# Moving a router's third token unit beside the attention chunks, and the row writes of four tile pairs back

## The chip, the cores and the metric

The kernel runs on one core of one Trainium2 chip. The core has five instruction queues that run on their own and meet only at semaphores: TensorE (PE in the profile, with its weight loads as PEld), VectorE (DVE), ScalarE (ACT), GpSimd (POOL) and SyncE (SP). The last three also issue the transfers. The metric is the device time of one execution in microseconds (us), as the median of several runs.

## The reference

Two blocks follow each other. The first is gated linear attention over 4 batches, 8 heads, 768 steps and head width 48; its state decays by `alpha` and takes up `k` times `v` at every step:

```python
state = alpha[:, :, t, :, None] * state + np.einsum('bhd,bhe->bhde', k[:, :, t], v[:, :, t])
y[:, :, t] = np.einsum('bhd,bhde->bhe', q[:, :, t], state)
```

Its output, as 3072 rows of 384 numbers, goes to a router with 8 experts. Each row gets noisy logits, `x @ w_gate + log(1 + exp(x @ w_noise)) * noise`; the two best experts are chosen, their softmax weights are the gates, and the row's result is the sum over its two experts of `gate * (relu(x @ w1[e]) @ w2[e])`, with w1 of 384 x 1024 and w2 of 1024 x 384. All of it is float32.

## The kernel before, in words

**Chunks.** The attention runs over 24 chunks of 128 rows, six to a batch. A loop of 23 turns (n from 0 to 22) issues for each turn the pieces of several chunks at different stages: keys, inverses, scaled keys and queries of chunk n + 2, alphas and products of n + 3, the transposed keys of n + 1, the output of n, the state and the masked scores of n + 1. The title of the change counts from 1, so its chunks 19 to 22 are the turns n = 18 to 21. In DVE's queue a turn is, in this order: the scan `over` (L385), the scaled queries `q_P` (L413), the state `S` (L472), two copies under a mask (L445, "masks" below; they write the matrix that L254 on PE multiplies with the values) and the scan `P_all` (L373). POOL multiplies the keys with `over` (L403, `k_P`) and decays the state (L473). The order of the pieces is written out by hand in a string:

```python
ORDER = "keys inverses alphas turn_y turn_k scaled queries block output no_more state scores masked products"
```

A place p of a turn is behind the p-th piece of this string.

**Routing.** The 24 chunks are four units of six. When a unit's chunks are done, `routing(u)` finds for its 768 rows the two best experts (DVE finds the 8 largest and their indices, L742 and L743, two chunks at a step), the gates (ACT: Exp, Ln, Exp, with table loads between), and each row's place in its expert's list. For the place PE multiplies the counts with a triangular and a full matrix of ones (L795, L796, `rank`). Then `enter` computes 12 columns of places (L801 to L820), and POOL writes 12 times 128 entries into a table in memory, one indirect transfer each (L173, "puts" below). The generator is stepped on by hand. `ROUTE[u]` lists for units 0 and 1 the (turn, place) of every step, counted from the turn in which the unit's last chunk is at its third stage; units 2 and 3 are stepped on by times in the second half.

**Pairs.** The second half is 24 pairs of tiles, 256 rows of one expert each, and three smaller tiles. A pair gathers its rows with an indirect transfer (L1008), turns them (PE, or a transposing transfer from pair 2 on), and multiplies them with the weights in fewer products than the plain form, with sums of blocks formed by DVE (L1229, L1232, L1290, L1381, L1385). ACT and DVE gather the result of pair i in `o`, of which there are two: pair i uses the one that pair i - 2 used. POOL writes the rows of `o` out with two plain indirect transfers (L992) and two that add (L1000). Pairs 0 to 4 read lists that units 0 and 1 alone fill; pair 5 needs unit 2, later ones all four.

**What sets the order in the second half.** Each step of a pair has a time on a scale on which a pair lasts T = 20, and all steps are sorted by it: this is the order in which they stand in each engine's queue, and it is no time on the chip. (d, t) below is d * T + t. A put of the second half also waits for the DVE sum that was recorded last before it (`behind`).

Of the kernel before, what the change touches and what calls it, by code (L numbers as in the profile page):

```python
# [19 lines left out]
def kernel(  # L20
# [273 lines left out]
    def fast_gla(on):  # L294
# [210 lines left out]

        ROUTE = (((1, 9), (2, 8), (2, 13), (3, 4), (3, 11), (4, 8), (4, 10), (4, 10), (5, 5), (5, 7)), ((1, 9), (2, 8), (2, 11), (2, 13), (3, 4), (3, 8), (3, 10), (3, 10), (4, 5), (4, 7), (4, 12)))
        routes = [routing(u, on) for u in range(NU)]

        def route(n, place):
            for u in range(2):
                for _ in range(ROUTE[u].count((n - (u + 1) * UC + 1, place))):
                    next(routes[u], None)

# [164 lines left out]
    seen = [const.tile([C, E], F32, name=f"seen{i}") for i in range(2)]  # L680
# [4 lines left out]
    def routing(u, on, planned=True):  # L685
        late = u if planned and u >= NU - 2 else 0
        noisy, lg = noisy_logits(u, on)
        yield
        nc.scalar.activation(noisy, noisy, AF.Ln, bias=1.0)
        yield  # L690
        top, at = best(u, on, lg, noisy, [])
        yield
        for c in range(0, UC - 2, 2):
            if (u, c) in ((NU - 2, 2), (NU - 1, 0)):
                nc.scalar.activation(unread_exp, ones[0:1, 0:1], AF.Exp)
            best(u, on, lg, noisy, range(c, c + 2), top, at)
            yield
        best(u, on, lg, noisy, range(UC - 2, UC), top, at)
        entry, at_f = choose(on, top, at)
        if u < NU - 2:  # L700
            nc.scalar.activation(unread_exp, ones[0:1, 0:1], AF.Exp)
            yield
        gates(entry)
        yield
        picked, counts = choose_rest(u, on, entry, at_f)
        past = count_past(u, on, counts)
        yield
        rank = ranked(u, on, counts, past)
# [53 lines left out]
    def choose_rest(u, on, entry, at_f):  # L762
        rp = on["two"]
        w = entry[:, :, :, 1]
        den = rp.tile([C, UC, 1], F32, name="den")
        nc.vector.tensor_add(den, w[:, :, 0:1], w[:, :, 1:2])
        nc.vector.tensor_scalar(out=den, in0=den, scalar1=1e-9, scalar2=None, op0=ALU.add)
        nc.vector.reciprocal(out=den, in_=den)
        nc.vector.tensor_mul(w, w, den.to_broadcast([C, UC, 2]))
        nc.gpsimd.tensor_copy(out=entry[:, :, :, 0], in_=token_f[:, ds(u * UC, UC), None].to_broadcast([C, UC, 2]))  # L770
        for k in range(2):
            nc.gpsimd.tensor_copy(out=entry[:, :, k, 2], in_=at_f[:, 1 - k, :])

# [7 lines left out]
        (nc.gpsimd if u < NU - 2 else nc.vector).tensor_copy(out=counts[:, :, 0], in_=seen[u % 2])  # L781
        chosen = counts[:, :, 1:].rearrange("p e c -> p c e")
        nc.vector.tensor_tensor(chosen, picked[:, 0], picked[:, 1], op=ALU.add)
        return picked, counts

    def count_past(u, on, counts):
        past = on["two"].tile([C, E, 1 + UC], F32, name="past")
        nc.vector.tensor_tensor_scan(past.rearrange("p e c -> p (e c)"), within.rearrange("p e c -> p (e c)"),
                                     counts.rearrange("p e c -> p (e c)"), 0.0, op0=ALU.mult, op1=ALU.add)
        (nc.gpsimd if u < NU - 2 else nc.vector).tensor_copy(out=seen[(u + 1) % 2], in_=past[:, :, UC])  # L790
        return past

    def ranked(u, on, counts, past):
        rank = few(on, [C, UC, E], "rank", u >= NU - 2)
        nc.tensor.matmul(rank, before, counts[:, :, 1:].rearrange("p e c -> p c e"), start=True, stop=False)  # L795
        nc.tensor.matmul(rank, ones, past[:, :, 0:UC].rearrange("p e c -> p c e"), start=False, stop=True)  # L796
        return rank
# [57 lines left out]
        nc.vector.tensor_scalar(out=short, in0=short, scalar1=float(R2), scalar2=None, op0=ALU.is_lt)  # L855

    def check_third(on):
        total = few(on, [C, E], "total", True)
# [264 lines left out]
    def pairs(on):  # L1123
# [17 lines left out]
        tabs, wheres, lists, bank, puts = {}, {}, {}, {}, {}  # L1141
# [262 lines left out]

        T = 20.0
        FIRST_BEHIND = 2
        PUT_LATER = {1: 13.0, 2: 16.0, 3: 12.0, 4: 6.0}
        EARLY_0 = {"tab": -300.0, "w1": -410.0, "find": -200.0, "gather": -199.0, "w2": -405.0, "join": -100.5, "turn": -100.0,
                   "turned": -100.0, "joined": -100.0, "s0": -1.05, "sum_x": -1.0, "sum_xs": -0.99, "s1": -0.8, "s3": -0.7, "s2": -0.6, "t0": 3.5, "t1": 4.3}
        every = {("w1", 0): 1.0, ("w2", 0): 1.0, ("w1", 1): 1.2, ("w2", 1): 2.0}  # L1410
# [309 lines left out]
    with ExitStack() as es:  # L1720
        on = pools(es, "")
# [8 lines left out]
        def beside():  # L1730
# [7 lines left out]
            left += [(t, lambda: route_on(2)) for t in when((0, 8.95), (0, 12.0), (0, 12.65), (0, 13.1), (0, 17.4), (0, 18.7), (0, 19.96), (1, 3.6), (1, 4.6), (2, 19.0))]  # L1738
            left += [(t, lambda: route_on(3)) for t in when((1, 5.0), (1, 10.2), (2, 5.2), (2, 7.6), (2, 9.7), (2, 9.8), (2, 12.2), (2, 15.2), (2, 17.5))]
            left += [(t, lambda: route_on(3)) for t in when((5, 10.7), (8, 10.7), (9, 1.6), (9, 6.2), (11, 10.7), (11, 20.8), (12, 1.6), (12, 6.2))]  # L1740
            puts = when((1, 6.0), (1, 8.6), (1, 10.1), (1, 12.7), (1, 14.0), (1, 16.6), (1, 19.2), (2, 0.6), (2, 2.6), (2, 5.2), (2, 9.0), (2, 11.4), (2, 17.6), (2, 18.9), (3, 2.6), (3, 3.9), (3, 5.2), (3, 6.5), (3, 8.8), (3, 10.1), (3, 11.4), (3, 12.7), (3, 15.0), (3, 17.3))
            left += [(t, lambda: put_some(1, latest["sum"])) for t in puts]
            assert len(puts) == 4 * UC
            return left

        steps = [pair_steps(i) for i in range(NPAIR)]
# [151 lines left out]
```

## Time and profile before

| | |
|---|---|
| Median of 3 runs | 620.96 us (620.77 to 621.24) |
| The profiled execution | 621.97 us |
| Its span, first to last instruction | 620.3 us |
| PE busy | 607.0 us, 98% |
| PE weight loads busy | 583.7 us, 94% |
| DVE busy | 508.0 us, 82% |
| ACT busy | 330.9 us, 53% |
| POOL busy | 317.4 us, 51% |
| Granted TensorE clock over the span | 0.997 |

The profiled execution is 1.0 us longer than the median. Times inside it are counted from the span's start. The chunks end and the pairs begin at about 153 us; the last products of the pairs end at about 613 us.

### The profile page before, as it was taken

The numbers are of one execution on the slowest core, as the hardware profiler recorded it, in microseconds if no ns is written. First come the engines' busy times: TensorE is split into PE (matmuls) and PEld (weight loads), VectorE is DVE, ScalarE is ACT, GpSimd is POOL, SyncE is SP. The second block draws the span as 40 slices with busy tenths as digits, with TensorE's granted clock in tenths as the row PEclk, the third lists the DMA queues.
The fourth block names the chain that finished last, engine by engine and source line by source line (L and its number), as shares of the span: only waits on it lengthen the run. The fifth ranks groups of instructions, "written<-read, shape, count | busy, mean of one in ns | idle before, by whom it ended". The sixth has DMA issues, their size and how long they took to land.

```text
span 620.3 us, 14271 instructions
## 1 busy us (share of the span) xinstructions
PE 607.0 (98%) x5274; PEld 583.7 (94%) x5274; DVE 508.0 (82%) x1158; ACT 330.9 (53%) x665; POOL 317.4 (51%) x355
## 2 busy tenths in 40 slices
PE   8999999999999999999999999999999999999994
PEld 5899999999999999999999999999999999989894
DVE  8788898988879869968898798887688879878672
ACT  4877868685655334444444544445544445444431
POOL 7353267884137786545434434555347527443254
PEclk9999999999999999999999999999999999999998
DMA  9999999984997854664654837775997678885223
GB/s 144 175 199 223 237 188 175 214 179 106 259 235 145 235 136 128 126 166 121 115 126 105 171 66 200 193 98 132 271 211 199 140 184 221 181 220 118 80 44 55
DMA packets 181552, 101.09 MB, mean 163 GB/s; under 512 B 150088, under 2 KB 172074, under 8 KB 181472
## 3 DMA queue, kind: packets, MB, share of 16 engines
q1 hardware_dynamic: 145056, 35.56, 34.5%
q10 hardware_dynamic: 21280, 44.05, 24.4%
q0 software_dynamic: 15136, 20.47, 14.8%
q8 instruction: 44, 0.72, 0.5%
q14 instruction: 36, 0.29, 0.2%
HBM read 76.41 MB, written 24.22 MB: 162 GB/s over the span
## 4 chain that ended last, share of the span: by engine, by line
PE 81%; DVE 6%; POOL 5%; issue 4%; ACT 2%; DMA 1%; POOLq 0%; ACTq 0%; DVEq 0%
PE sc L1356 19%; PE h_ps L1363 18%; PE o_ps L1363 13%; PE c_ps L1356 8%; PE sc L1348 4%; PE tp L345 3%; PE sc L425 3%; PE y L254 2%; PE h_ps L277 2%; POOL table L173 2%; PE y L493 2%; DVE P_all L373 1%; POOL k_P L403 1%; PE tp L452 1%; PE h_half_ps L1678 1%
## 5 line engine op out<-in xcount | busy, mean ns | idle before, releaser
L992 POOL DMA_INDIRECT out_dram<-o,where x46 | 48.5, 1054 | 166.6 <-DVE o L1381 91.1
L1367 ACT ACTIVATE h<-h 128x512 f32<-128x512 f32 x92 | 56.9, 628 | 78.2 <-DVE h L1229 61.7
L1000 POOL DMA_INDIRECT out_dram<-o,where x44 | 71.0, 1615 | 13.4 <-issue 13.1
L1008 POOL DMA_INDIRECT x_in<-x_rows,where x48 | 58.6, 1220 | 24.4 <-issue 12.7
L1363 PE MATMUL o_ps<-wt,hx 128*128 128x192 f32 x384 | 70.8, 327 | 0.0
L1356 PE MATMUL sc<-yT,ws 128*128 128x128 f32 x480 | 66.6, 275 | 1.5 <-DVE m L1232 1.5
L1356 PEld LDWEIGHTS sc<-yT,ws 128*128 128x128 f32 x480 | 62.9, 191 | 1.8 <-DVE m L1232 1.8
L173 POOL DMA_INDIRECT table<-entry,place_u x48 | 55.0, 1145 | 16.5 <-issue 9.5
L1363 PEld LDWEIGHTS o_ps<-wt,hx 128*128 128x128 f32 x384 | 61.5, 190 | 1.8 <-issue 1.8
L403 POOL TENSOR_TENSOR k_P<-k_P,over 128x512 f32<-128x512 f32 (+1 forms) x24 | 27.7, 1154 | 40.5 <-DVE over L385 32.3
L1223 ACT COPY xt<-x_turned 128x768 uint16<-128x768 uint16 x44 | 43.8, 1053 | 2.1 <-DMA x_turned<-x_in 2.1
L345 PE MATMUL tp<-ident,ins 128*128 128x128 f32 x288 | 42.9, 282 | 1.6 <-ACT k_P L395 0.6
L1377 ACT ACTIVATE o<-h_ps,tab 128x192 f32<-128x192 f32 x46 | 19.4, 421 | 42.7 <-PE h_ps L1363 41.3
L345 PEld LDWEIGHTS tp<-ident,ins 128*128 128x128 f32 x288 | 32.1, 144 | 7.1 <-ACT k_P L395 1.0
L445 DVE COPY_PREDICATED shared<-upto,sc 128x512 f32<-128x512 uint32 x47 | 32.0, 736 | 7.6 <-PE sc L425 7.0
L1488 ACT COPY m<-sc 128x512 f32<-128x512 f32 x20 | 11.7, 586 | 48.0 <-PE sc L1356 48.0
L1363 PE MATMUL h_ps<-wt,h 128*128 128x192 f32 x192 | 35.2, 327 | 0.0
L1363 PE MATMUL o_ps<-w,h 128*128 128x192 f32 x192 | 35.2, 326 | 0.0
L1363 PE MATMUL h_ps<-wt,hx 128*128 128x192 f32 x192 | 35.2, 326 | 0.0
L1363 PE MATMUL h_ps<-w,h 128*128 128x192 f32 x192 | 35.1, 326 | 0.0
L1363 PE MATMUL h_ps<-w,hx 128*128 128x192 f32 x192 | 35.1, 326 | 0.0
L1356 PE MATMUL c_ps<-xs,w 128*128 128x128 f32 x240 | 33.3, 275 | 0.0
(333 smaller groups left out, 1611.9 us busy)
## 6 DMA issues: line engine op xcount, KB each, us to landing
w<-in_moe_w_dram ACTq DMA_DIRECT2D x33, 512.0 KB
w<-in_moe_w_dram ACTq DMA_DIRECT2D x44, 384.0 KB
ins<-in_alpha_dram SPq DMA_DIRECT2D x24, 192.0 KB
ins<-in_k_dram SPq DMA_DIRECT2D x24, 192.0 KB
ins<-in_q_dram SPq DMA_DIRECT2D x24, 192.0 KB
vt<-in_v_dram SPq DMA_DIRECT2D x24, 192.0 KB
x_rows<-y_sb SPq DMA_DIRECT2D x24, 192.0 KB
ins<-in_moe_w_dram ACTq DMA_DIRECT2D x9, 512.0 KB
```

The lines of the kernel that those rows point to most:

```text
L173: put = nc.gpsimd.indirect_dma_start(out=table, out_offset=bass.IndirectOffsetOnAxis(ap=place, axis=0), in_=entry, in_offset=None, bounds_ ...
L345: nc.tensor.transpose(tp[:, j, :], src[:, 2 * j:2 * j + 2, :], ident)
L403: (nc.vector if n == NT - 1 else nc.gpsimd).tensor_tensor(c["k"][:, at], c["k"][:, at], over[:, at, 1:CB], op=ALU.mult)
L445: nc.vector.copy_predicated(MTs[n % 2][:, i], mask_upto, sc)
L992: put = nc.gpsimd.indirect_dma_start(out=out, out_offset=bass.IndirectOffsetOnAxis(ap=at, axis=0), in_=rows, in_offset=None, bounds_check= ...
L1000: add = nc.gpsimd.indirect_dma_start(out=out, out_offset=bass.IndirectOffsetOnAxis(ap=at, axis=0), in_=rows, in_offset=None, bounds_check= ...
L1008: nc.gpsimd.indirect_dma_start(out=rows, out_offset=None, in_=x_rows[0:units * UT, :], in_offset=bass.IndirectOffsetOnAxis(ap=at, axis=0), ...
L1223: nc.scalar.copy(halves[:, part], x_turned[:, :, part].rearrange("p s a t -> p s (a t)"))
L1348: nc.tensor.matmul(bank[name][:, f, :], W[:, ds(f * C, C)], X, start=new and f == 0, stop=True, skip_group_check=True)
L1356: nc.tensor.matmul(bank[name][:, 2 * h + f, :], W[h][:, ds(f * C, C)], X[h], start=new and not h and not f, stop=True, skip_group_check=True)
L1363: nc.tensor.matmul(bank[name], H[:, f, :], W[:, f, :], start=new and f == 0, stop=True, skip_group_check=True)
L1367: nc.scalar.activation(t, t if src is None else src, AF.Relu)
```

## The change

Unit 2 gets a row of its own in `ROUTE`, the same as that of unit 1, so that its eleven steps stand in turns 18 to 21. The ten times at which it was stepped on in pairs 0 to 2 now step unit 3 on; nine are left, and the nine times of unit 3 in pairs 1 and 2 are gone. Where the code asked whether a unit is one of the last two (`u < NU - 2`) it now asks whether it is the last, so unit 2 takes its rank bank from the pool `h`, copies its counts on POOL, and loads the Exp table where units 0 and 1 do. Of unit 2's 12 puts four go in turns 21 and 22 (`put_some(2)` was there and had nothing left to put), eight at eight new times in pair 0. Unit 3's 12 puts take the first twelve of the 24 old times. `PUT_LATER`, by which the row writes of pairs 1 to 4 stood 6 to 16 units later than those of other pairs, is empty.

```diff
-        ROUTE = (((1, 9), ..., (5, 7)), ((1, 9), (2, 8), (2, 11), ..., (4, 12)))
+        ROUTE = (((1, 9), ..., (5, 7)), ((1, 9), (2, 8), (2, 11), ..., (4, 12)), ((1, 9), (2, 8), (2, 11), (2, 13), (3, 4), (3, 8), (3, 10), (3, 10), (4, 5), (4, 7), (4, 12)))
...
-            for u in range(2):
+            for u in range(NU - 1):
...
-            if (u, c) in ((NU - 2, 2), (NU - 1, 0)):
+            if (u, c) == (NU - 1, 0):
...
-        if u < NU - 2:
+        if u < NU - 1:
             nc.scalar.activation(unread_exp, ones[0:1, 0:1], AF.Exp)
             yield
...
-        rank = few(on, [C, UC, E], "rank", u >= NU - 2)
+        rank = few(on, [C, UC, E], "rank", u >= NU - 1)
...
-        PUT_LATER = {1: 13.0, 2: 16.0, 3: 12.0, 4: 6.0}
+        PUT_LATER = {}
...
-            left += [(t, lambda: route_on(2)) for t in when((0, 8.95), (0, 12.0), ..., (1, 4.6), (2, 19.0))]
-            left += [(t, lambda: route_on(3)) for t in when((1, 5.0), (1, 10.2), ..., (2, 17.5))]
+            left += [(t, lambda: route_on(3)) for t in when((0, 8.95), (0, 12.0), ..., (1, 4.6))]
...
-            puts = when((1, 6.0), (1, 8.6), ..., (2, 11.4), (2, 17.6), ..., (3, 17.3))
+            puts = when((0, 0.5), (0, 2.0), ..., (0, 11.0), (1, 6.0), (1, 8.6), ..., (2, 11.4))
...
-            assert len(puts) == 4 * UC
+            assert len(puts) == 4 * UC - 4
```

DVE in turn 20, from the scan `over` of chunk 22 to the masks of chunk 21 (`sc` with two numbers); L1182 begins the row search of pair 0. Before:

```order
L385 SCALAR_TENSOR_TENSOR over<-shared,P_all 128x515
L413 TENSOR_TENSOR q_P<-tp,P_all 128x512
L472 TENSOR_TENSOR S_156<-S_155,o_ps 128x192
L445 COPY_PREDICATED shared<-upto,sc_2352 128x512
L445 COPY_PREDICATED shared<-upto,sc_2353 128x512
L1182 TENSOR_SCALAR tab_2279<-tab_2279 128x2
```

Now there stand three steps of the largest values behind `over`, and behind them, up to the masks:

```order
L754 TENSOR_TENSOR entry<-top 128x12
L766 TENSOR_TENSOR den<-entry 128x6
L767 TENSOR_SCALAR den<-den 128x6
L768 RECIPROCAL den<-den 128x6
L769 TENSOR_TENSOR entry<-entry,den 128x12
L776 TENSOR_TENSOR picked<-expert_idv,at_f 128x96
L783 TENSOR_TENSOR counts<-picked 128x6x8
L788 SCALAR_TENSOR_TENSOR past<-within,counts 128x56
L472 TENSOR_TENSOR S_156<-S_155,o_ps 128x192
L445 COPY_PREDICATED shared<-upto,sc_2396 128x512
L445 COPY_PREDICATED shared<-upto,sc_2397 128x512
```

The state and the masks of chunk 21 stand behind six searches for the largest values, the gates' sums and the counts of unit 2.

DVE in turn 21, from the scan `over` of chunk 23 over the masks of chunk 22. Before:

```order
L385 SCALAR_TENSOR_TENSOR over<-shared,P_all 128x515
L403 TENSOR_TENSOR k_P<-k_P,over 128x512
L472 TENSOR_TENSOR S_155<-S_156,o_ps 128x192
L445 COPY_PREDICATED shared<-upto,sc_2443 128x512
L445 COPY_PREDICATED shared<-upto,sc_2444 128x512
L413 TENSOR_TENSOR q_P<-tp,P_all 128x512
```

Now:

```order
L385 SCALAR_TENSOR_TENSOR over<-shared,P_all 128x515
L403 TENSOR_TENSOR k_P<-k_P,over 128x512
L801 TENSOR_TENSOR picked<-picked,h_ps 128x96
L803 TENSOR_REDUCE place_f<-picked 128x12
L815 TENSOR_SCALAR picked<-place_f 128x2x6
L817 TENSOR_TENSOR picked<-place_f,picked 128x2x6
L820 SCALAR_TENSOR_TENSOR place_u<-at_f,picked 128x12
L472 TENSOR_TENSOR S_155<-S_156,o_ps 128x192
L445 COPY_PREDICATED shared<-upto,sc_2499 128x512
L445 COPY_PREDICATED shared<-upto,sc_2500 128x512
L860 SCALAR_TENSOR_TENSOR short<-h_ps,short 128x1
L413 TENSOR_TENSOR q_P<-tp,P_all 128x512
```

The five instructions of `enter` for unit 2 stand ahead of the state and the masks of chunk 22, and the check of one list's length (L860) behind them.

POOL in pairs 2 and 3, where the rows of pair 1 (`o_186`) and of pair 2 (`o_185`) are written out; L1155 loads a list of three pairs. Before:

```order
L173 DMA table<-entry,place_u 25600x8 x6
L1008 DMA x_in<-x_rows,where_3175 128x768 x2
L173 DMA table<-entry,place_u 25600x8
L992 DMA out_dram<-o_186,where_2463 3072x384
L1000 DMA out_dram<-o_186,where_2463 3072x384
L173 DMA table<-entry,place_u 25600x8
L992 DMA out_dram<-o_186,where_2463 3072x384
L1000 DMA out_dram<-o_186,where_2463 3072x384
L173 DMA table<-entry,place_u 25600x8 x4
L1155 DMA tab_3365<-table 128x6x8
```

Now:

```order
L173 DMA table<-entry,place_u 25600x8 x2
L992 DMA out_dram<-o_186,where_2522 3072x384
L1000 DMA out_dram<-o_186,where_2522 3072x384
L992 DMA out_dram<-o_186,where_2522 3072x384
L1000 DMA out_dram<-o_186,where_2522 3072x384
L1008 DMA x_in<-x_rows,where_3205 128x768 x2
L992 DMA out_dram<-o_185,where_2651 3072x384
L1000 DMA out_dram<-o_185,where_2651 3072x384
L992 DMA out_dram<-o_185,where_2651 3072x384
L1000 DMA out_dram<-o_185,where_2651 3072x384
L1155 DMA tab_3377<-table 128x6x8
```

Of twelve puts in this stretch two are left, ahead of the four row writes of pair 1; the writes of pair 2 now stand ahead of the list.

## Rows read from the trace of the kernel before

**Rows 1.** Windows: stretch, length, busy PE, PEld, DVE, ACT, POOL, clock, DMA, GB/s.

```profile
229.00:242.00 13.00, 11.23 (x87) 10.77 (x86) 10.51 (x21) 5.93 (x11) 8.00 (x8) 1.00 0.40 106
242.00:600.00 358.00, 358.00 (x2717) 349.29 (x2716) 292.28 (x670) 171.02 (x300) 170.63 (x135) 1.00 0.65 153
```

**Rows 2.** Timeline of PE and ACT in pairs 3 and 4: start, us, what, [idle before].

```profile
230.36 1.47 PE L1363 MATMUL h_ps<-wt,hx 128*128 128x192 f32 x8
230.97 0.42 ACT L1377 ACTIVATE o<-o_ps,tab 128x192 f32<-128x192 f32 x1 [3.86 <-DMA out_dram<-o,where]
...
233.36 1.16 PE L1356 MATMUL sc<-yT,ws 128*128 128x128 f32 x8 [1.54 <-DVE m L1232]
...
235.25 1.47 PE L1363 MATMUL h_ps<-wt,h 128*128 128x192 f32 x8
...
236.55 0.61 PE L1356 MATMUL sc<-yT,ws 128*128 128x128 f32 x4
...
240.93 0.68 PE L1356 MATMUL sc<-xt,q_P 128*128 128x128 f32 x4 [0.23 <-ACT h L1367]
```

**Rows 3.** Timeline of DVE where unit 1 is routed, turn 14.

```profile
101.35 1.23 DVE L385 TENSOR_TENSOR_SCAN over<-shared,P_all 128x515 f32<-128x515 f32 x1
102.50 0.14 DVE L742 MAX8 top<-noisy 128x8 f32<-128x8 f32 x1
...
103.17 0.67 DVE L413 TENSOR_TENSOR q_P<-tp,P_all 128x512 f32<-128x512 f32 x1
...
108.25 1.22 DVE L373 TENSOR_TENSOR_SCAN P_all<-shared,least 128x516 f32<-128x516 f32 x1
```

**Rows 4.** Timeline of DVE and POOL in turns 19 to 22.

```profile
135.54 1.37 DVE L445 COPY_PREDICATED shared<-upto,sc 128x512 f32<-128x512 uint32 x2 [0.62 <-issue]
...
136.50 1.21 POOL L403 TENSOR_TENSOR k_P<-k_P,over 128x512 f32<-128x512 f32 x1
...
136.79 2.02 DVE L373 TENSOR_TENSOR_SCAN P_all<-shared,least 128x516 f32<-128x516 f32 x1
...
139.13 1.23 DVE L385 TENSOR_TENSOR_SCAN over<-shared,P_all 128x515 f32<-128x515 f32 x1
...
143.59 0.15 DVE L1182 TENSOR_SCALAR tab<-tab 128x2 f32<-128x2 f32 x1
...
144.14 1.22 DVE L373 TENSOR_TENSOR_SCAN P_all<-shared,least 128x516 f32<-128x516 f32 x1
...
149.12 0.68 DVE L413 TENSOR_TENSOR q_P<-tp,P_all 128x512 f32<-128x512 f32 x1
```

**Rows 5.** Timeline of PE: output products of chunks 21 and 22.

```profile
145.04 1.09 PE L254 MATMUL y<-shared,vt 128*48 128x128 f32 x16
...
149.98 1.09 PE L254 MATMUL y<-shared,vt 128*48 128x128 f32 x16
```

**Rows 6.** Timeline of DVE: `enter` of unit 2 in pair 1, first instruction and the next.

```profile
180.46 0.26 DVE L801 TENSOR_TENSOR picked<-picked,rank 128x96 f32<-128x96 f32 x1
...
181.56 0.25 DVE L722 TENSOR_TENSOR lg<-lgs 128x96 f32<-128x96 f32 x1
```

**Rows 7.** Timeline of PE: rank of unit 1 in turn 15.

```profile
106.52 0.44 PE L795 MATMUL h_ps<-counts,before 128*128 128x48 f32 x2
...
107.16 0.62 PE L345 MATMUL tp<-ident,ins 128*128 128x128 f32 x4
```

**Rows 8.** Timeline of PE: rank of unit 2 in pair 1.

```profile
179.85 0.34 PE L795 MATMUL rank<-counts,before 128*128 128x48 f32 x2
...
180.24 1.12 PE L1348 MATMUL sc<-xt,ws 128*128 128x128 f32 x8
```

**Rows 9.** Timeline: gather of pair 2's rows, and first reading of them turned.

```profile
159.41 1.00 POOL L1008 DMA_INDIRECT x_in<-x_rows,where  x1 [5.88 <-ACT x_turned L288]
...
178.75 1.06 ACT L1223 COPY xt<-x_turned 128x768 uint16<-128x768 uint16 x1
```

**Rows 10.** Waits of PE: us in total, times, longest.

```profile
PE tp L345 <- DVE q_P L413: 0.4, 2, 0.2
```

More of the change, by code (lines that the diff above doesn't have):

```diff
@@ L504, in put_y @@
                 put_rows(n, chunks[n].pop("y"))
-        ROUTE = (((1, 9), (2, 8), (2, 13), (3, 4), (3, 11), (4, 8), (4, 10), (4, 10), (5, 5), (5, 7)), ((1, 9), (2, 8), (2, 11), (2, 13), (3, 4), (3, 8), (3, 10), (3, 10), (4, 5), (4, 7), (4, 12)))
+        ROUTE = (((1, 9), (2, 8), (2, 13), (3, 4), (3, 11), (4, 8), (4, 10), (4, 10), (5, 5), (5, 7)), ((1, 9), (2, 8), (2, 11), (2, 13), (3, 4), (3, 8), (3, 10), (3, 10), (4, 5), (4, 7), (4, 12)), ((1, 9), (2, 8), (2, 11), (2, 13), (3, 4), (3, 8), (3, 10), (3, 10), (4, 5), (4, 7), (4, 12)))
         routes = [routing(u, on) for u in range(NU)]
         def route(n, place):
-            for u in range(2):
+            for u in range(NU - 1):
                 for _ in range(ROUTE[u].count((n - (u + 1) * UC + 1, place))):
@@ L780, in choose_rest @@
         counts = rp.tile([C, E, 1 + UC], F32, name="counts")
-        (nc.gpsimd if u < NU - 2 else nc.vector).tensor_copy(out=counts[:, :, 0], in_=seen[u % 2])
+        (nc.gpsimd if u < NU - 1 else nc.vector).tensor_copy(out=counts[:, :, 0], in_=seen[u % 2])
         chosen = counts[:, :, 1:].rearrange("p e c -> p c e")
@@ L789, in count_past @@
                                      counts.rearrange("p e c -> p (e c)"), 0.0, op0=ALU.mult, op1=ALU.add)
-        (nc.gpsimd if u < NU - 2 else nc.vector).tensor_copy(out=seen[(u + 1) % 2], in_=past[:, :, UC])
+        (nc.gpsimd if u < NU - 1 else nc.vector).tensor_copy(out=seen[(u + 1) % 2], in_=past[:, :, UC])
         return past
     def ranked(u, on, counts, past):
-        rank = few(on, [C, UC, E], "rank", u >= NU - 2)
+        rank = few(on, [C, UC, E], "rank", u >= NU - 1)
         nc.tensor.matmul(rank, before, counts[:, :, 1:].rearrange("p e c -> p c e"), start=True, stop=False)
@@ L857, in check_third @@
     def check_third(on):
-        total = few(on, [C, E], "total", True)
+        total = few(on, [C, E], "total")
         nc.tensor.matmul(total, ones, seen[(NU - 1) % 2], start=True, stop=True)
@@ L1737, in beside @@
             when = lambda *steps: [d * T + t for d, t in steps]
-            left += [(t, lambda: route_on(2)) for t in when((0, 8.95), (0, 12.0), (0, 12.65), (0, 13.1), (0, 17.4), (0, 18.7), (0, 19.96), (1, 3.6), (1, 4.6), (2, 19.0))]
-            left += [(t, lambda: route_on(3)) for t in when((1, 5.0), (1, 10.2), (2, 5.2), (2, 7.6), (2, 9.7), (2, 9.8), (2, 12.2), (2, 15.2), (2, 17.5))]
+            left += [(t, lambda: route_on(3)) for t in when((0, 8.95), (0, 12.0), (0, 12.65), (0, 13.1), (0, 17.4), (0, 18.7), (0, 19.96), (1, 3.6), (1, 4.6))]
             left += [(t, lambda: route_on(3)) for t in when((5, 10.7), (8, 10.7), (9, 1.6), (9, 6.2), (11, 10.7), (11, 20.8), (12, 1.6), (12, 6.2))]
-            puts = when((1, 6.0), (1, 8.6), (1, 10.1), (1, 12.7), (1, 14.0), (1, 16.6), (1, 19.2), (2, 0.6), (2, 2.6), (2, 5.2), (2, 9.0), (2, 11.4), (2, 17.6), (2, 18.9), (3, 2.6), (3, 3.9), (3, 5.2), (3, 6.5), (3, 8.8), (3, 10.1), (3, 11.4), (3, 12.7), (3, 15.0), (3, 17.3))
+            puts = when((0, 0.5), (0, 2.0), (0, 3.5), (0, 5.0), (0, 6.5), (0, 8.0), (0, 9.5), (0, 11.0), (1, 6.0), (1, 8.6), (1, 10.1), (1, 12.7), (1, 14.0), (1, 16.6), (1, 19.2), (2, 0.6), (2, 2.6), (2, 5.2), (2, 9.0), (2, 11.4))
             left += [(t, lambda: put_some(1, latest["sum"])) for t in puts]
-            assert len(puts) == 4 * UC
+            assert len(puts) == 4 * UC - 4
             return left
```

## The prediction

> **What bounds the kernel now.** I read the page's busy shares first, then the windows by stage, then PE's own waits, then the timelines around the two places that the change touches. PE is busy for 98% of the span at the full clock, so only a stretch in which PE stands still can give time back, and everything that makes PE stand still somewhere else costs time. The windows tell where it stands still. From 242 to 600 us PE is busy for all 358 us; from 229 to 242 it is busy for 11.23 of 13 [rows 1]. The reader is to see there that the second half has one hole, and that nothing in the pairs after pair 4 is to be had.
>
> The hole is in pairs 3 and 4. ACT's first write into `o` for pair 3 waits 3.86 us, until 230.97, for the transfer that still reads that `o`: the rows of pair 1 [rows 2]. POOL has 12 puts in that stretch, and the old `PUT_LATER` puts the row writes of pair 1 among them. DVE's sum of pair 4 comes late behind ACT, and PE's step at 233.36 waits for it. Eight products of that shape take 1.30 us (235.25 to 236.55), the eight before the hole take 3.00 (230.36 to 233.36), so 1.70 are lost. A second wait of 0.23 stands at 240.93 [rows 2], where DVE has not caught up; busy rows overhang the next start by 1.47 - 1.30 = 0.17, so it is 0.40. Together 2.1 us. The idle shown in the windows, 1.77, is the floor of this term.
>
> **The change part by part.** *Row writes and puts.* With the puts gone from pairs 2 and 3 and the writes of pair 1 directly behind its last sums, POOL is done with them before pair 3 comes to write, and ACT finds `o` free. I take the whole 2.1 as gained, with 1.8 as the lower end. Nothing takes the hole's place as the next to be late: the windows show no second one behind it.
>
> *Unit 2 beside the chunks.* This costs DVE time in a stage where DVE has little. I follow DVE from turn 19 to the output of chunk 22. The two noise sums of unit 2 stand before the masks of chunk 20, where DVE sits idle for 0.62 [rows 4], and the sum of the logits in a like gap one turn before: nothing. The first step of largest values takes 0.67, as the one between 102.50 and 103.17 for unit 1 [rows 3], and pushes the scan `P_all` at 136.79 to 137.46. That scan took 2.02 before, against 1.22 for the same scan at 144.14; it began 0.29 after POOL's `k_P`, with 0.92 of that to go [rows 4]. Moved, it shares only 0.25 with it. So of the extra 0.80 between none and all may go; I take 0.55, since the overlap shrinks by about that share. `over` then starts at 139.13 + 0.67 - 0.55 = 139.25 (139.0 to 139.8).
>
> What follows `over` is now what followed it for unit 1: two steps of largest values, the entry, the wait for the gates, the counts, the state and the masks. There it took from 101.35 to 108.25, 6.90 us [rows 3]. So the masks of chunk 21 end at 146.15; before they ended at 143.59, where the row search begins [rows 4]. PE wants them at 145.04 [rows 5], had a slack of 1.45, and the masks come 2.56 later. PE has to wait until 146.2, which is 1.15 later than before. The rank products of unit 2 lie inside this: in turn 15 they took 0.64 [rows 7], and PE would have come at 145.68 with them.
>
> The next masks are worse. From the end of the masks of chunk 21 to the end of those of chunk 22 DVE had no gap to speak of: 143.59 to 149.12, 5.53 us [rows 4]. Five instructions of `enter` now stand in between, 1.10 us from 180.46 to 181.56 [rows 6]. So these masks end at 146.15 + 6.63 = 152.8. PE multiplies with them at 149.98 [rows 5], and now at 152.85: 2.9 us later than before. The product that checks a list lies in this wait. From here PE and DVE are late by the same amount: the scaled queries of chunk 23 follow the masks directly, and pair 0's first sums wait for PE's scores as before. So the loss at the chunks is 2.9 us. Its ends: `over` at 139.0 and at 139.8 give 2.6 and 3.4.
>
> *What leaves the pairs.* PE no longer computes the rank of unit 2 in pair 1, 0.39 from 179.85 to 180.24 [rows 8], nor the small check, for which I take half of that: 0.6. DVE's and ACT's part of unit 2 in pairs 0 and 1 does not leave; unit 3's takes its place at the same times. Unit 3's in pairs 1 and 2 does leave, some 6 us of DVE, and gives nothing where PE is never waiting.
>
> *Moved for nothing.* Two puts stand in each of turns 21 and 22 behind the state on POOL; behind them wait the gathers of pairs 0 and 1, which PE sees only through DVE's copies of the rows, and these come later anyway. Five puts now stand ahead of pair 2's gather, at 159.41 before; such a transfer took POOL 1.00 there, so with their issue they are 5 to 7 us. The turned rows are first read at 178.75 [rows 9], so 19 us cover the gather, its landing and the transposes. Were that cover gone, PE would stand at pair 2 for what is over. Unit 3's column copies on POOL still stand ahead of pair 0's row writes, and wait for DVE at the same place as unit 2's did. The table loads of ACT are as many as before.
>
> *The sum.* + 2.9 - 0.6 - 2.1 = + 0.2 us. On the profiled execution's own time, 621.97, that is 622.2. That execution is 1.0 above the median of the runs, so the forecast for the median is 621.2 us. The likeliest case's own range is 620.5 to 622.2.
>
> **A rule that bears on the scans.** The scan at 136.79 reads two arrays from the local memory while POOL's product does so too, and takes 0.80 longer [rows 4]. The Trainium skill, SBUF - State Buffer, "Who interferes with whom", says that a DVE instruction with two such inputs and a GpSimd instruction that reads there exclude each other: the one issued second waits until the first is done. The trace agrees within 0.12 us (0.80 against the 0.92 left). By the rule the moved scan would wait 0.25, so 0.55 would be won, as taken; without it the sum would be + 0.75. It also speaks against the change, and that is the second rival's mechanism.
>
> **The rivals.** *DVE keeps up, and it is faster.* Unit 1 stands at the same places in its turns, and all that PE ever waited for DVE's scaled queries is 0.4 us in two waits [rows 10]. If unit 2 costs PE no more than this and the products, 0.4 + 0.64 + 0.2 (the check), the sum is 1.24 - 0.6 - 2.1 = - 1.5: 619.5 us. For it: the same list of places, and gaps of DVE in turns 18 to 20 that unit 1 did not have. Against it: turns 21 and 22 are shorter for PE, which has fewer chunks left to prepare, while DVE has the row searches of two pairs and the scaled keys of chunk 23 on top; that is what the 5.53 shows.
>
> *DVE and POOL block each other in turns 21 and 22, and it is slower.* POOL now has five column copies for unit 2, the states and the puts in the stretch where DVE runs `P_all` and `over` of chunk 23. If each of these scans is stretched as the one at 136.79, by 0.80 [rows 4], the masks of chunk 22 come 1.6 later and PE with them: 622.8 us. It decides from 1.0 us of stretching on, one scan in full and a quarter of the other. For it: DVE is on the path there without slack, so that each stretch counts in full. Against it: POOL's gather runs beside the scan at 144.14 in the old order without stretching it, and the states are short.
>
> *The hole stays.* If ACT's wait for `o` is not due to the order of POOL but to how slowly the adding transfers land, the 2.1 do not come back: 623.3 us. Against it: the same transfers of later pairs, without puts, hold nobody up from 242 us on [rows 1].
>
> **How the numbers follow.** The forecast 0.58, DVE keeps up 0.15, blocking 0.21, the hole stays 0.06. A measurement of this kernel tells about 0.2%, 1.24 us, from no change: below 619.72 is faster, above 622.20 slower. The forecast lies well inside and gives its chance to no change, with the little that its own range has at the upper edge going to slower; the first rival gives 0.15 to faster, the others give theirs mostly to slower: 0.15 faster, 0.60 the same, 0.25 slower. The range takes in the first rival and the second, and leaves out the third: 619.4 to 622.9.
>
> **What would show it.** Right would be: no wait of ACT for `out_dram` in pair 3, PE without a gap from 229 to 242 us on the old scale; PE waiting at L254 or at the rank in turn 21 for 0.5 to 1 us and at L254 in turn 22 for 1.2 to 1.8 us, both for DVE's masks; the products of pair 0 beginning 2.6 to 3.4 us later than before, and the last ones ending within a microsecond of before. Wrong would be: PE's waits in turns 21 and 22 below 0.8 us together, or above 3.3; a new wait in pairs 0 to 2, for pair 2's rows above all; or a wait for `o` that is still there.

## The result and the profile after

The changed kernel took 624.37 us in the median (623.27 to 625.99), the kernel before 620.99 (620.40 to 621.63): a ratio of 1.0057, 95% interval 1.0042 to 1.0073. It is slower by 3.4 us where 0.2 were forecast, and lies outside the range.

The profiled execution of after took 624.09 us. Both ends of the sum can be read from when PE starts the same product in both traces. At the first product of pair 0 the new kernel is 6.60 us late, at the last product of all 3.65: 6.60 lost beside the chunks, where 2.9 were forecast, and 2.95 won in the pairs, where 2.7 were. (The profiled execution of before is 1.0 us above its own median, so the difference of the medians is the better measure of the whole.)

What was won is as forecast. In the windows of after (stretch, length, busy PE, PEld, DVE, ACT, POOL, clock, DMA, GB/s) the hole of [rows 1], which lies some 4 to 6 us later here, is full:

```profile
235.00:250.00 15.00, 15.00 (x119) 15.00 (x118) 14.69 (x33) 6.87 (x12) 2.55 (x3) 1.00 0.44 121
250.00:600.00 350.00, 350.00 (x2656) 341.30 (x2655) 286.94 (x656) 167.44 (x294) 165.31 (x131) 1.00 0.66 154
```

and of ACT's wait for `o`, 3.86 us in [rows 2], the waits of after (total, times, longest) keep

```profile
ACT o L1377 <- DMA out_dram<-o,where: 0.7, 1, 0.7
```

What was lost stands in DVE's timeline of turns 19 to 22, which answers to [rows 4] (start, length, what, and the idle time before it):

```profile
136.42 1.39 DVE L737 TENSOR_TENSOR noisy<-noisy,noise 128x48 f32<-128x48 f32 x1 [1.47 <-ACT noisy L689]
137.84 0.42 DVE L738 TENSOR_TENSOR noisy<-noisy,lg 128x48 f32<-128x48 f32 x1
138.19 1.34 DVE L445 COPY_PREDICATED shared<-upto,sc 128x512 f32<-128x512 uint32 x2
...
141.64 1.23 DVE L385 TENSOR_TENSOR_SCAN over<-shared,P_all 128x515 f32<-128x515 f32 x1
...
147.53 1.34 DVE L445 COPY_PREDICATED shared<-upto,sc 128x512 f32<-128x512 uint32 x2
148.76 0.16 DVE L1182 TENSOR_SCALAR tab<-tab 128x2 f32<-128x2 f32 x1
...
154.09 1.36 DVE L445 COPY_PREDICATED shared<-upto,sc 128x512 f32<-128x512 uint32 x2
155.34 0.14 DVE L860 SCALAR_TENSOR_TENSOR short<-h_ps,short 128x1 f32<-128x1 f32 x1
```

The masks of chunk 20 start at 138.19, where they started at 135.54 [rows 4]: 2.65 late before any step of largest values has run. DVE waited 1.47 us for the Ln, and then a sum that takes 0.2 elsewhere took 1.39. From there the chain runs as forecast: of the three steps of the largest values one stands ahead of `P_all` and two behind `over`, as the prediction has it (the text on the change puts all three behind `over`); `over` to the end of the masks of chunk 21 takes 7.12 us (6.90 forecast), and from there to the end of those of chunk 22 6.58 (6.63).

Why the Ln was late is in the timeline of ACT and POOL:

```profile
131.11 1.74 POOL L173 DMA_INDIRECT table<-entry,place_u  x1 [0.17 <-issue]
132.87 1.22 POOL L473 TENSOR_TENSOR S<-S,P_end 128x192 f32<-128x192 f32 x1
...
134.12 0.71 ACT L479 COPY S_block<-S 64x192 f32<-64x192 f32 x2 [1.70 <-POOL S L473]
134.85 1.28 ACT L689 ACT_TABLE_LOAD   x1
136.15 0.24 ACT L689 ACTIVATE noisy<-noisy 128x48 f32<-128x48 f32 x1
...
136.53 1.21 POOL L403 TENSOR_TENSOR k_P<-k_P,over 128x512 f32<-128x512 f32 x1
```

POOL puts entries of unit 1's list ahead of the state; ACT waits 1.70 us for that state with `S_block`, and the Ln with its table load of 1.28 us stands behind `S_block`. DVE's sum then meets POOL's `k_P`, and ends 0.07 behind it. Before had the same wait of `S_block` (1.70 us, to 134.09), and behind it only the copy to `yT`, which PE read at 136.37 without a wait.

PE in turns 21 and 22, and the windows around, answer to [rows 5]:

```profile
144.20 1.15 PE L277 MATMUL h_ps<-to_rows,yT 128*128 128x112 f32 x8 [1.00 <-ACT yT L496]
...
147.05 0.66 PE L795 MATMUL h_ps<-counts,before 128*128 128x48 f32 x2 [1.27 <-DVE counts L783]
...
147.94 2.03 PE L493 MATMUL y<-q_P,S_block 128*128 128x128 f32 x8
149.91 1.95 PE L254 MATMUL y<-shared,vt 128*48 128x128 f32 x16
...
156.58 1.09 PE L254 MATMUL y<-shared,vt 128*48 128x128 f32 x16
...
160.29 0.96 PE L1348 MATMUL sc<-xt,w 128*128 128x128 f32 x7
```

```profile
142.00:146.00 4.00, 2.77 (x28) 2.18 (x24) 3.31 (x18) 3.24 (x8) 1.84 (x6) 1.00 0.42 100
146.00:150.00 4.00, 2.95 (x14) 2.73 (x16) 3.76 (x16) 2.21 (x7) 1.16 (x3) 0.55 0.15 55
150.00:154.00 4.00, 4.00 (x49) 3.77 (x49) 3.69 (x10) 0.78 (x2) 2.88 (x4) 0.59 0.29 69
```

PE waits for the rank, and behind that its clock is granted at 0.55 and 0.59 on the mean of two windows, a stretch at the lower of its two levels (1.2 and 2.4 GHz): the products of L493 took 2.03 us for the 1.07 that they take at 155.58. L254 of chunk 22 starts 1.1 us after the masks that it needs.

So three suspects came out of this trace: the late Ln (2.65), the work itself (the forecast's 2.9) and the clock.

### The profile page after: what moved, and what is told of

Its sections match the earlier page's. It is cut to its first block, busy times and chain, and to the rows that moved or that the text cites. A ratio compares the mean times of both kernels' runs of the same rounds, so it can differ in the third digit from the quotient of the medians.

```text
span 622.5 us, 14273 instructions
## 1 busy us (share of the span) xinstructions
PE 610.3 (98%) x5274; PEld 586.5 (94%) x5274; DVE 508.6 (82%) x1156; ACT 330.0 (53%) x665; POOL 316.6 (51%) x357
## 4 chain that ended last, share of the span: by engine, by line
PE 86%; DVE 7%; ACT 2%; POOL 2%; issue 2%; POOLq 0%; DVEq 0%; ACTq 0%
PE sc L1356 20%; PE h_ps L1363 19%; PE o_ps L1363 14%; PE c_ps L1356 9%; PE sc L1348 5%; PE tp L345 3%; PE sc L425 3%; PE y L254 3%; PE h_ps L277 2%; PE y L493 2%; DVE P_all L373 1%; DVE over L385 1%; DVE shared L445 1%; PE o_ps L467 1%; PE h_half_ps L1678 1%
```

## The experiments

Eight chips were met. On three of them (that of the recorded result among them) before took 620.65 to 621.0 us; on five it took 630.5 to 632.9, and there PE stops for no reason that the profile shows (at the end of this section). I call them the quiet and the stopping chips. The terms of the sum are sized on quiet ones. Lateness is always PE's start of a product in a run, less the start of the same product in the profiled execution of before. The edits below are shortened where they have dots or comments.

**The row writes alone.** Edit to before:

```diff
-        PUT_LATER = {1: 13.0, 2: 16.0, 3: 12.0, 4: 6.0}
+        PUT_LATER = {}
```

> Before, with the row writes of pairs 1 to 4 in their old places as the one edit; the third unit's routing and all 24 list puts stay in the pairs. Theory (the late row writes alone made the hole at 233.36 and 240.93, which held 1.70 + 0.40 us): TensorE has no wait left in pairs 3 and 4, the last TensorE instruction comes 2.0 to 2.2 sooner, 618.9 us (ratio 0.9966). Rival (the list puts still in pairs 1 to 3 now stand where the row writes and gathers do, so the hole moves to another pair or the gathers of pair 3 come late): 620.5 to 623 us, with a wait of TensorE for xt or o somewhere in 190 to 300 us.

> Before with the row writes of pairs 1 to 4 in their old places, on the same chip as its neighbours. Theory (the late row writes made the hole): 1.70 + 0.50 us less at 233.36 and 240.93, 618.5 to 619 us, ratio 0.9966 as on one chip so far. Rival: 620.5 us or above.

The first (e1), on a stopping chip, gave 0.999 of before's time (0.9954 to 1.0025), and the same kernel on a second (e1b) 0.9987 (0.9938 to 1.0035): neither tells it from before. On a third (e7) it gave 0.9969 (0.9949 to 0.9988), and on a quiet chip (f2) 618.37 us, 0.9967 (0.9949 to 0.9984), where 618.5 to 619 were expected. There its windows show the hole full:

```profile
229.00:242.00 13.00, 13.00 (x101) 13.00 (x100) 12.75 (x24) 6.24 (x11) 9.95 (x8) 1.00 0.60 156
```

PE is 0.04 us early up to 228.57 us of before and 2.31 early at 245.38. The row writes alone give the whole gain, with all 24 puts left in the pairs. The reverse edit, after with the row writes late again:

> After, with the row writes of pairs 1 to 4 late again by 13, 16, 12 and 6 places as before. Theory (the row writes' places alone made the hole): it is back, 1.70 + 0.40 us of TensorE waits in pairs 3 and 4, 626.5 us. Rival (the list puts in pair 3 made it, and they are gone there): 624.4 us, no wait.

1.0018 (0.9987 to 1.0049) on a stopping chip. Its trace has ACT's wait for `out_dram` at 0.8 us, and PE's lateness falls from 16.36 at 228.57 to 14.09 at 245.38, by 2.27 as in after. So the hole is gone here too, against my expectation: with the puts out of pairs 2 and 3 POOL is at the row writes in time even at their late places. It takes both, late row writes and puts among them, to make the hole; taking away either one is enough.

**After again, and before on the same kind of chip.**

> The kernel before, profiled on the chip on which the variants run, since one chip gave 632.2 us for it and another 621.0. Theory (the difference lies in TensorE's own stops, which the variants' traces of that chip show at 155 to 159 and at 199 to 208 us with no semaphore in front of them): on the chip of 621 us none; on the chip of 632 us some 10 us of such stops here too. Rival (the stops come with the edits): none on either chip.

> The kernel after once more, so that it stands on one chip with the variants. Theory (the loss is VectorE's lateness in turns 19 to 22, 6.6 us at the first product of pair 0, and 2.2 us come back where the hole was): ratio 1.004 to 1.007 on the quiet chip; the clock falls to 0.5 near 146 us. Rival (the fall of the clock is chance): the same chain of VectorE with the clock at 1.0, and pair 0 starting 5.4 to 6.1 us late.

> The kernel after once more, on the same chip as its neighbours. Theory: VectorE's chain repeats (masks of chunk 22 end at 155.4 where the Ln is late, 154.2 where TensorE stopped in turn 17 and it is not), and the fall of the clock near 146 us is not in every execution: without it pair 0 starts near 159.1 as in the variant with the Ln later, 1.2 us sooner than the 160.29 of the first trace. Ratio 1.004 to 1.007. Rival (the clock falls whenever these waits stand there): 0.5 at 146 to 153 again.

b2 and a2 fell on a stopping chip: 633.65 us, and 1.0007 (0.9964 to 1.0049). f3, on the quiet chip of f2, gave 625.77 us, 1.0081 (1.0060 to 1.0103): the loss repeats. Its chain of DVE repeats too, and its clock does not fall:

```profile
136.10 1.40 DVE L737 TENSOR_TENSOR noisy<-noisy,noise 128x48 f32<-128x48 f32 x1 [1.47 <-ACT noisy L689]
...
155.02 0.14 DVE L860 SCALAR_TENSOR_TENSOR short<-h_ps,short 128x1 f32<-128x1 f32 x1
```

```profile
146.00:150.00 4.00, 3.26 (x44) 3.03 (x44) 3.79 (x15) 2.16 (x6) 1.47 (x3) 1.00 0.16 55
```

**The Ln.** Edits to the third list of `ROUTE` in after, one place at a time:

```diff
-((1, 9), (2, 8), (2, 11), (2, 13), (3, 4), ...
+((1, 9), (2, 7), (2, 11), (2, 13), (3, 4), ...    # e2, e6, f1: the Ln ahead of S_block
+((1, 9), (2, 9), (2, 11), (2, 13), (3, 4), ...    # d1: the Ln behind the copy to yT
+((1, 9), (2, 8), (2, 13), (2, 13), (3, 4), ...    # d2: the sums behind the masks of chunk 20
```

> After, with the third unit's Ln one place sooner (place 7 of turn 19 in the stead of 8), so that its table load of 1.28 us stands ahead of the ACT copy that waited 1.70 us for POOL's S. Theory (the late Ln made the chain of VectorE 2.6 us late, and TensorE's clock fell to 0.5 because of the waits that followed): VectorE's wait of 1.47 us for the Ln is gone, masks of chunk 22 end at about 152.8 in the stead of 155.34, the clock stays at 1.0, and the time is 2.6 + 1.2 less: 620.6 us. Theory with the clock apart (it falls in any case where TensorE waits for counts and yT): 621.8 us, clock 0.5 still seen. Rival (VectorE has too much work in turns 20 and 21 whatever the Ln does): 624.0 to 624.4 us, and the wait for the Ln is replaced by one for the sc of TensorE or a later start of the masks at the same end.

> After with the third unit's Ln one place sooner, again. On the two chips so far TensorE stood still for 1 to 2 us near 127 us in every trace, so that VectorE was late in turn 19 for that reason and the Ln was in time even where it was not moved (Ln at 136.00, sums at 136.27 for 0.21 us): the theory of the late Ln could not show there. Theory of the Ln, on a chip without that stop: VectorE's wait of 1.47 us is gone, masks of chunk 22 end at about 152.8 to 153.5, pair 0 starts 3.5 to 4.5 us later than before in the stead of 6.6, 621 to 622 us. Rival (VectorE's work alone): pair 0 starts 6 us or more late. On a chip with the stop both say the same as for after: masks of chunk 22 near 154.2.

> After, with the third unit's Ln one place later (behind the copy to yT in turn 19), since on the chips of these runs the Ln was in time: this makes it as late as it was in the first trace of after. Theory (a late Ln holds VectorE's sums, and with them all masks behind them, one for one): Ln at about 138.2 in the stead of 136.00, VectorE idle 1.5 to 2 us in front of the sums, masks of chunk 20 end 1.5 to 2.1 later than 138.25 and masks of chunk 22 as much later than 154.16, product L254 of turn 22 at about 155.7. Rival (slack in turns 20 to 22 takes it up): masks of chunk 22 within 0.3 of 154.16. If TensorE's stand that grows by this brings the clock down, a stretch at 0.5 shows between 142 and 156.

> After, with the third unit's two noise sums behind the masks of chunk 20 in the stead of ahead of them. Theory (VectorE's work in turns 20 and 21 sets the end, and in these runs the Ln is in time): masks of chunk 20 end about 1.0 sooner, masks of chunk 22 0 to 0.5 sooner than 154.16, pair 0 starts within 0.5 of 159.6. Rival (the place of the sums made the whole loss): masks of chunk 22 at 152 or before.

> After with the third unit's Ln one place sooner, for a chip on which TensorE runs turn 17 undisturbed, as in the recorded run of after. Theory: Ln done at about 134.2 in the stead of 136.39, no wait of VectorE for it (1.47 us in after), masks of chunk 20 end at 136.9 to 137.3 in the stead of 139.53, masks of chunk 22 at 152.9 to 153.3 in the stead of 155.45, clock at 1.0, pair 0 starts at 156.6 to 157.1 (before: 153.69, after: 160.29); 621 us, ratio 1.000 to 1.002. Rival (the sums beside POOL's k_P are stretched wherever they stand): masks of chunk 22 at 154.2 as with the sums behind the masks, pair 0 at 158.0.

e2 (1.0019, 0.9992 to 1.0046) and e6 (1.0004, 0.9971 to 1.0036) fell on stopping chips, where PE was already about 1 us late at 135.44 and DVE with it: masks of chunk 22 end at 154.16 and 154.50, as in a2 (154.16). In a2 the Ln is in time for a DVE that is late itself: the sum starts without a wait at 136.27 and takes 0.21. There was nothing to gain there. On quiet chips f1 gave 622.29 us, 1.0034 (1.0017 to 1.0051), 3.5 us less than after on the same chip, where 621 were expected. Its DVE, PE and ACT:

```profile
134.84 0.20 DVE L737 TENSOR_TENSOR noisy<-noisy,noise 128x48 f32<-128x48 f32 x1
...
135.54 1.38 DVE L445 COPY_PREDICATED shared<-upto,sc 128x512 f32<-128x512 uint32 x2 [0.26 <-PE sc L425]
...
151.57 1.34 DVE L445 COPY_PREDICATED shared<-upto,sc 128x512 f32<-128x512 uint32 x2
152.80 0.14 DVE L860 SCALAR_TENSOR_TENSOR short<-h_ps,short 128x1 f32<-128x1 f32 x1
```

```profile
152.56 1.49 PE L254 MATMUL y<-shared,vt 128*48 128x128 f32 x16
...
156.66 1.07 PE L1348 MATMUL sc<-xt,w 128*128 128x128 f32 x8
```

```profile
132.42 1.28 ACT L689 ACT_TABLE_LOAD   x1
133.72 0.24 ACT L689 ACTIVATE noisy<-noisy 128x48 f32<-128x48 f32 x1
134.08 0.71 ACT L479 COPY S_block<-S 64x192 f32<-64x192 f32 x2
```

One place sooner the table load fills ACT's wait to the tenth, `S_block` does not move (134.08 for 134.12), and the masks of chunk 20 start at 135.54 as before. `P_all`, moved to 137.49, takes 1.30 us (1.47 by the forecast). The masks of chunk 22 end at 152.91 (forecast 152.8), L254 starts at 152.56 (152.85), pair 0 is 2.98 late (2.9). This is the forecast's chain, met once the Ln is in time.

d1 gave 627.18 us, 1.012 (1.0069 to 1.0171). Its Ln came at 136.66, only 0.5 later, and the wait grew to 2.08; but the first sum ended with `k_P` as in after and the second at 138.18 for 138.26, so the masks came no later than there: the expected 1.5 to 2.1 on top did not come, since `k_P` held DVE in after already. Nor did the clock fall. d2 gave 623.68 us, 1.0042 (1.0002 to 1.0081): the masks of chunk 20 end at 136.85, as before, those of chunk 22 at 154.25, since the sums, now at 136.74, still run into `k_P`:

```profile
136.74 1.00 DVE L737 TENSOR_TENSOR noisy<-noisy,noise 128x48 f32<-128x48 f32 x1
```

**The clock.** After with products that nobody reads in two of PE's waits of turn 21:

```diff
+            idle(bank, 3 * C)              # ahead of L277 of chunk 20
+            idle(held_bank.pop(), 4 * C)   # ahead of the rank of unit 2
```

> After, with products of 384 and 512 columns that nobody reads added in two waits of TensorE in turn 21: ahead of the row products L277 (which waited 1.00 us for yT) and ahead of the rank (which waited 1.27 us for counts). Theory (the fall of the granted clock to 0.5 from 146.4 to 153.3 costs 1.2 us beyond what VectorE's masks cost): with the clock at 1.0 the product L254 of turn 22 waits for the masks of chunk 22 that end at 155.34, and starts at about 155.4 in the stead of 156.58; 623.2 us. Rival (VectorE alone sets the end): 624.4 us with the clock at 1.0. Rival (the fall comes of something else): the clock falls all the same, 624.4 us or above.

1.0007 (0.9979 to 1.0034) on a stopping chip, where the clock did not fall at these places without them either (a2): it tells nothing. f3 and d1 tell it: the same masks of chunk 22 (155.12 and 155.36, after 155.45) at full clock. PE's lateness in us, by the product's start in before:

| | 135.44 | 149.98, L254 of chunk 22 | 153.69, pair 0 | 165.39 | 228.57 | 245.38 |
|---|---|---|---|---|---|---|
| after, clock falls | 0.03 | 6.61 | 6.60 | 6.60 | 5.94 | 3.66 |
| f3, after again | -0.29 | 4.79 | 5.18 | 6.29 | 5.62 | 3.35 |
| d1, Ln later | -0.06 | 5.03 | 5.42 | 6.61 | 7.88 | 5.60 |
| f1, Ln sooner | 0.01 | 2.58 | 2.98 | 4.12 | 3.55 | 1.28 |
| f4, values only | -0.37 | -0.39 | 0.18 | 0.18 | 0.18 | -2.10 |
| f2, rows alone | -0.02 | -0.04 | -0.04 | -0.04 | -0.04 | -2.31 |

With the column of 135.44 taken off, the fall of the clock costs 1.1 us at the start of pair 0, and at 165.39 nothing is left of it: the traces without it lose 1.1 to 1.2 inside pair 0. So it does not explain the time. (d1 loses 1.8 more between 180 and 190 us, as on a stopping chip.)

At the last product the lateness is 3.65 in after, 4.46 in f3 and 1.58 in f1: f3 loses 1.1 more between 400 and 500 us and f1 0.3, in a stretch where the two programs are the same, and nothing here says why. So of the 3.5 us between the times of f3 and f1 the traces give the Ln 2.1 at 245.38, or 2.4 with the column of 135.44 taken off. The medians say as much: after is 3.4 above before in the recorded result, f1 is 1.4 above before on its own chip.

**The work.** After with the Ln sooner, and unit 2's choice, counts, rank, entries and check out of the turns. e5 puts them behind the last masks and in pairs 0 and 1, f4 where before has them, with unit 3's steps and the 24 puts of before as well:

```diff
-..., (3, 4), (3, 8), (3, 10), (3, 10), (4, 5), (4, 7), (4, 12))
+..., (3, 4), (3, 13), (4, 4), (5, 13))    # e5
+..., (3, 4), (3, 13), (4, 4))             # f4
+route_on(2) at (0, 8.95), (0, 12.0), (1, 3.2)                  # e5
+route_on(2) at (0, 19.96), (1, 3.6), (1, 4.6), (2, 19.0)       # f4
```

> After with the Ln one place sooner, and with only the third unit's logits, Ln, largest values and gates beside turns 18 to 22: the choice and counts stand behind the masks of the last chunk, the rank, the entries and the check in pair 0 and 1, and the 24 puts in pairs 0 to 2. Theory (VectorE's 4.6 us of the third unit in turns 20 and 21, not the Ln alone, hold TensorE): about 2.9 us of VectorE's work leave the two turns, pair 0 starts 0.5 to 1.5 us later than before in the stead of 6.6, the hole stays gone, 619 to 620 us (ratio 0.997 to 0.9985). Rival (the Ln and the clock alone made the loss): no better than the variant with the Ln sooner, pair 0 still 3 us or more late, 621 us or above.

> Before with the row writes in their old places, and with only the third unit's logits, Ln (one place sooner), largest values and gates beside turns 18 to 22; choice, rank, entries, check and all 24 puts at their places of before. Theory (VectorE's work on the third unit in turns 20 and 21 made the loss, 2.9 us of it the choice, counts, entries and check): the product L254 of turn 22 starts 0.7 to 1.1 later than before, pair 0 1.0 to 1.5 later, the hole is gone: 619.5 to 620.5 us, ratio 0.998 to 0.999. Rival (any of the third unit's work beside the chunks costs as much as all of it): pair 0 starts 4 us or more late, 622 us.

e5, on a stopping chip, gave 1.0198 (1.0132 to 1.0264): its puts stand in two dense runs, and PE stops beside and behind both. But L254 of chunk 22 starts at 150.70 there, where a2 has 153.81 and b2 149.75 on the same chip. f4, on the quiet chip of f1 to f3, gave 618.83 us, 0.9964 (0.9950 to 0.9978), better than the 619.5 to 620.5 expected. PE:

```profile
150.16 1.08 PE L254 MATMUL y<-shared,vt 128*48 128x128 f32 x14 [0.16 <-DVE shared L445]
...
153.86 1.07 PE L1348 MATMUL sc<-xt,w 128*128 128x128 f32 x8
```

Pair 0 starts 0.18 late, 0.55 if its head start of 0.37 is counted. In f1 the same two numbers are 2.98 and 2.97. So the sums, the largest values and the gates' Exp of unit 2 cost about 0.5 us beside the chunks, and the choice, counts, rank, entries and check with their puts, which f4 leaves out there, the other 2.4 of the 2.9.

**The puts ahead of the gather.** f1 meets the forecast up to pair 0 and then loses 1.14 more by 165.39. POOL and ACT of f1 in pair 0:

```profile
154.00 1.31 POOL L173 DMA_INDIRECT table<-entry,place_u  x1 [0.31 <-issue]
155.61 1.04 POOL L1008 DMA_INDIRECT x_in<-x_rows,where  x1 [0.30 <-issue]
156.96 1.04 POOL L1008 DMA_INDIRECT x_in<-x_rows,where  x1 [0.30 <-issue]
...
161.06 1.06 ACT L288 COPY x_turned<-x_in 128x768 uint16<-128x768 uint16 x1
163.97 1.06 ACT L288 COPY x_turned<-x_in 128x768 uint16<-128x768 uint16 x1 [1.84 <-DMA x_in<-x_rows,where]
...
165.51 1.15 PE L277 MATMUL h_ps<-to_rows,yT 128*128 128x112 f32 x8 [0.32 <-ACT yT L496]
```

Two puts stand ahead of the gather on POOL's queue; ACT's second copy of the rows waits 1.84 us for it, and the copy to `yT`, which PE needs, stands behind. Edit to f1: all puts back at the places of before.

> After with the third unit's Ln one place sooner, and with all its 12 list puts (and the fourth unit's) back at the places that before has in pairs 1 to 3; the row writes stay in their old places. In the trace with the Ln sooner, 0.5 and 0.7 us more were lost at 162 and 165 us of the program before (PE h_ps <- ACT yT, behind ACT's wait of 1.8 us for the gather x_in; PE sc <- DVE h). Theory (the two puts ahead of the gather on POOL's queue made the gather late, and that the 1.1 us): pair 0 starts 3.0 us later than before as it did there, no more is lost up to 180 us, the hole stays gone since the row writes are in their old places: 621.2 us, ratio 1.0005. Rival (VectorE and ACT are late in pair 0 whatever POOL does): 622.3 us as with the Ln sooner.

> After with the Ln sooner and the puts of the third and fourth unit back in pairs 1 to 3, once more, for a chip on which TensorE does not stop beside runs of list puts. Theory (Ln 2.2 to 2.5 us and puts ahead of the gather 1.1 us were what the forecast missed): pair 0 starts 3.0 us later than before, nothing more is lost in it, 0.7 comes back with rank and check and 2.2 with the hole: 621.0 us, ratio 1.000. Rival (something else holds pair 0): 622.3 us as with the puts sooner.

Both fell on stopping chips: 1.000 (0.9967 to 1.0034) and 0.9968 (0.9927 to 1.0009), so the expected 621 us could not be seen. The step could. In the trace of g1 ACT's copies run without a wait,

```profile
156.46 1.10 POOL L1008 DMA_INDIRECT x_in<-x_rows,where  x1 [2.59 <-DVE x_turned L288]
...
162.64 1.97 ACT L288 COPY x_turned<-x_in 128x768 uint16<-128x768 uint16 x2
```

and the lateness grows by 0.24 and 0.28 us from 153.69 to 165.39 (f1: 1.14). b2, before on a stopping chip, grows by 0.27 over the same stretch. So 0.9 to 1.1 us of it are the puts.

**The stopping chips.** In all their traces, that of before (b2) included, PE pauses inside rows of like products with nothing in front (`issue`). PE of b2:

```profile
196.30 1.16 PE L1348 MATMUL sc<-xt,ws 128*128 128x128 f32 x8 [2.07 <-issue]
...
199.27 0.80 PE L1363 MATMUL h_ps<-wt,h 128*128 128x192 f32 x2 [1.09 <-issue]
200.69 0.80 PE L1363 MATMUL h_ps<-wt,h 128*128 128x192 f32 x2 [0.62 <-issue]
202.12 0.80 PE L1363 MATMUL h_ps<-wt,h 128*128 128x192 f32 x2 [0.63 <-issue]
```

These pairs of products start 1.4 us apart; in before, at 198.01, eight products of this shape take 1.47 us together. In b2 this comes to 12.6 us by 203.73 of before, beside and behind nine list puts in a row (187.11 to 199.27). The clock is not the start of it: it is granted in full from 190 to 196 us, where the first stop begins, and falls behind that (0.81 from 196 to 200, 0.50 from 200 to 212), which adds to the 12.6. In e5, whose puts stand elsewhere, PE stops from 184 to 195 and from 212 to 226 us, beside and behind its two runs of puts; in g1 and g2, with the puts of before, it does not stop at the nine in a row (192 to 205 us) but from 210 us on, beside later puts and row writes. So the puts alone do not set the place. What stops PE stays open.

## Why the prediction was wrong

*The hole: right.* 2.1 forecast, 2.3 measured (5.94 less 3.66). The prediction took the row writes and the puts together; the row writes' places alone do it (f2), and so do the puts alone (e3).

*Rank and check leave the pairs: right.* 0.6 forecast; 0.66 in after (6.60 less 5.94), and 0.67 in f3 and f1 between 180 and 228.57 us.

*DVE's chain: right in length, wrong in its start.* The step that failed reads: "The two noise sums of unit 2 stand before the masks of chunk 20, where DVE sits idle for 0.62 [rows 4] ...: nothing." I looked at DVE's gap alone. The sums need the Ln, the Ln its table, and both stand on ACT behind a copy that waits 1.70 us for POOL, a wait that cost nothing before and was no row of mine; of ACT's table loads I counted only that they "are as many as before", not where they stand. Then the sums slid into POOL's `k_P`. Cost: 2.5 us at the masks of chunk 22 (155.45 less 152.91), shown by taking it away in f1, whose time is 3.5 us below after's on the same chip; 2.0 to 2.4 of that are the Ln's by medians and traces. Of the difference between forecast and result this is the larger part.

*"Moved for nothing": wrong by about 1 us.* I wrote that PE sees the gathers "only through DVE's copies of the rows, and these come later anyway". One of the copies is ACT's, and `yT` stands behind it. By f1 against g1 and g2 the puts ahead of the gather are worth 0.9 to 1.1 us. In the recorded execution they cost nothing (PE is 6.60 late at 153.69 and at 165.39): ACT's two copies of the rows run there without a wait, at 164.69. That this is so because the fall of the clock had just made PE late by as much is argued from the table, not tried.

*The rivals.* DVE keeps up: no, only with choice and entries left out (f4). DVE and POOL block each other by stretched scans in turns 21 and 22: no. `over` at 141.64 took 1.23, as long as anywhere, and the scans of chunk 23, `P_all` at 149.32 and `over` at 150.79, 1.23 each; the blocking came two turns sooner, at a sum of 48 columns, which ended 0.07 to 0.08 us behind `k_P` in after, f3, d1 and d2 alike, whenever it had begun (in e6 and g1 it ended 0.07 behind the state that POOL ran next, L473). The Trainium skill, SBUF — State Buffer, "Who interferes with whom", says that a DVE instruction with two inputs in the local memory contends with a GpSimd instruction that reads there, for ports that only one can hold at a time. These traces agree: the sum of 0.20 us took 0.78 to 1.40 beside `k_P`. The hole stays: no. That the result is slower, as the second rival has it, is so by other steps than the rival's.

*Taken together* for after: 2.9 for the work, 2.5 for the Ln, 1.1 for the clock or, without its fall, for the puts ahead of the gather, less 0.7 and 2.3: 3.5 us late, against 3.65 at the last product and 3.4 in the medians. What the clock does to the time of a single execution stays untried, since e4 ran where the clock stayed up without the added products.

The best versions are before with its row writes back in place, 618.37 us, and f4, 618.83, whose runs overlap with it; none of unit 2's routing needs to move for the gain.

## What to carry to other kernels

When work is put into the idle time of one engine, follow each of its inputs back over the other engines and look there for waits that are harmless today: whoever is queued behind one inherits it. If an engine waits in order, put the new step (here a table load) ahead of the instruction that waits, where it costs nothing. And when two edits come together, price them apart: here the smaller edit alone gives the gain, and all of the loss came with the other.

## What the runs showed of the hardware

The same program's granted clock fell to 0.5 for 6.8 us in one execution (windows at 0.55 and 0.59) and not in another, with PE waiting at the same places for as long (1.00 and 1.27 us in after, 1.02 and 1.27 in f3, all windows from 142 to 154 us at 1.00). DVE's row for the sum in after starts 0.11 us ahead of POOL's for `k_P`, and it was the sum that ended last, by 0.07: the start of a row does not tell which of the two waits. An Ln whose table load of 1.28 us stands ahead of a copy that waits 1.70 us for POOL does not make that copy later (134.08 for 134.12). The same kernel took 620.65 to 621.0 us on three chips and 630.5 to 632.9 on five, each met once, with stops of TensorE on the five that no row explains.
